# Linear attention followed by a gated MLP: fewer dummy matmuls and another VectorE order in the prologue, and phi(q) of batch 1 taken in the given layout ahead of full-width transposes

## The chip, the cores and the metric

The kernel runs on one core of one Trainium2 chip. The metric is the device time of one execution in microseconds.

## The reference, cut to what matters

```python
# q, k, v: (8, 8, 576, 64) float32
def phi(x):
    return np.where(x > 0, x, np.exp(x) - 1.0) + 1.0      # = max(x, 0) + min(exp(x), 1)
q_p, k_p = phi(q), phi(k)
kv  = np.einsum('bhsd,bhse->bhde', k_p, v)
z   = np.sum(k_p, axis=2)
num = np.einsum('bhsd,bhde->bhse', q_p, kv)
den = np.einsum('bhsd,bhd->bhs', q_p, z)[..., None] + 1e-06
x   = (num / den).transpose(0, 2, 1, 3).reshape(4608, 512)
g   = x @ w_gate                                          # 512 -> 1536
out = ((g * sigmoid(g)) * (x @ w_val)) @ w_out            # 1536 -> 512
```

## The kernel before: what the change and the argument touch

Tokens are worked off in nine groups of 512, "layer 1" being gate and value (L292), "layer 2" the output product (L299). Batch 0's attention has no matmuls of another group to hide behind: it is the prologue. Batch 1's is woven into layer 2 of the first group. TensorE needs q with the features on the partitions, so q is transposed on TensorE. For batch 0 that is a matmul against the identity into PSUM that already holds 1, then an exponential and one VectorE operation from PSUM:

```python
WARM = (4, 3, 4, 4, 2, 1, 2, 2)        # dummy matmuls of a constant at eight places
def warm(n, w=512, ps=None):           # L124
    for _ in range(n):
        nc.tensor.matmul(out=(ps or pp4[1][1])[:, 512 - w:512], lhsT=ones[:, :],
                         rhs=ones[:, 0:1].to_broadcast([P, w]), start=True, stop=True)
# ... prologue; exp_* run on ScalarE, mx_/mn_/add_/q_phi/zr_copy/r_copy on VectorE
    q_turn(0, qa)                      # L430, 16 half-width turns
    q_exp(0, 0, qa)
    q_exp(0, 1, qa)
    warm(WARM[1])
    q_turn(1, qb)
    q_exp(1, 0, qb)
    q_exp(1, 1, qb)
    warm(WARM[2])
    exp_k(0, 0)
    exp_k(0, 1)
    q_phi(0, 0, qa)                    # L442, 128x512 from PSUM
    q_phi(0, 1, qa)
    mx_k(0, 0)                         # L143, 128x1152
    q_phi(1, 0, qb)
    mn_k(0, 0)                         # L147, 128x1152
    mx_k(0, 1)
    zt(0, 0, X[1], kp, True, False)    # L396, column sums of kp on TensorE, 9 matmuls
    warm(WARM[3])
    zt(0, 0, X[1], ek, False, True)    # column sums of ek: need mn_k(0, 0)
    zr_copy(0, 0, X[1])                # L400
    warm(WARM[4])
    t_corners(0, Zr, 0, pp4[2])        # denominators
    lnrd(pp4[2], 0)                    # 1/den by Ln and Exp on ScalarE
    mn_k(0, 1)
    q_phi(1, 1, qb)
    zt(0, 1, Y[0], kp, True, False)
    warm(WARM[5])
    zt(0, 1, Y[0], ek, False, True)
    add_k(0, 0)                        # L159, 128x1152
    zr_copy(0, 1, Y[0])
    warm(WARM[6])
    kv_corner(0, 0, kp, True, True)    # L185
    # ... r_copy, the second half, xT, then layer 1
```

For batch 1, raw q is transposed in 64-column halves and phi is taken after, from PSUM:

```python
    def qtr(b, lp, ps):                                      # L371, 16 halves
        pt = ps[:, :].bitcast(FP16).rearrange("p (j c) -> p j c", c=P)
        for j in range(J - 1):
            for l2 in range(2):
                nc.tensor.transpose(out=pt[D * l2:D * l2 + D, j, :],
                                    in_=qr[b][:, 2 * lp + l2, D * j:D * j + D], identity=id16[:, :])
    def t_phi(a, ps):
        return (lambda: act(a, ps, AF.Exp),
                lambda: nc.vector.tensor_scalar(out=a, in0=a, scalar1=1.0, scalar2=None, op0=ALU.min),
                lambda: nc.vector.scalar_tensor_tensor(out=a, in0=ps, scalar=0.0, in1=a,
                                                       op0=ALU.max, op1=ALU.add))   # L385
    # ... layer2_0
        def s0(): qtr(1, 0, cq[0]); exp_k(1, 1); pm[0][0](); mn_k(1, 1); add_k(1, 1)
                  zsum(1, 1, 2); pm[0][1](); pm[0][2]()
        def s1(): # qtr8 (L379, 8 halves of the ninth slot, both batches), then their phi
        def s3(): qtr(1, 1, cq[1]); pm[1][0]()
        def s5(): p1_z(); pm[1][1](); pm[1][2]()
        step = {1: [s0], 4: [s1, s3], 5: [s5]}
        for fb in range(9):
            for f in step.get(fb, []): f()
            for t in range(4): l2_mm(0, t, fb)               # L299
        s4()                                                 # L254: denominators of batch 1
```

(The step functions are shortened to one line each, and `s4`, which holds the denominators, is only named.)

## Time and profile before

| | before |
|---|---|
| time, median of 3 | 315.97 us (315.6 to 316.2) |
| span of the profiled run | 314.1 us |
| TensorE busy | 307.5 us, 98% |
| VectorE, ScalarE busy | 205.5 us (65%), 152.0 us (48%) |
| start of layer 1's long run of L292 | 19.64 us |
| first L299 of layer 2, and first L299 after the denominators L254 | 36.91 and 46.99 us |

The lines themselves stand in the prediction below. They are to be read thus. A TensorE that is busy for 98% leaves 2%: 2.4 us of it in the first 15 us, and 4.1 us after 309 us, when only the last tiles and the last store are left. But in the prologue TensorE is fed with dummies, so the busy share says nothing there. What sets the time there is the chain of work: each line of it gives a start, a length and what ran, and each piece began when the one above released it. Two numbers of the chain: the start of the column sums on `ek` (L396, L398 after the change), called E, and the start of layer 1's long run of L292, called L.

### The profile page before, as it was taken

Reading aid. Unit: us, or ns where it says so; the run is one execution under the profiler, and the core shown is the slowest. Engines: PE = TensorE matmul, PEld = TensorE weight load, DVE = VectorE, ACT = ScalarE, POOL = GpSimd, SP = SyncE. Lnnn points to the kernel's source line nnn. Section 1 sums busy time; section 2 is a strip of 40 time slices with the busy share of each in tenths; the row PEclk is TensorE's granted clock in tenths of the full one; section 3 lists DMA queues with packets and bytes.
Section 4 is the critical chain, followed back from the end, with each engine's and each line's share of the span. In section 5 each row is a group of like instructions: output and inputs, shape, how many; then the busy total and the mean of one; then the engine's idle time right before and its main releaser. Section 6 shows DMA issues by size and latency. Waiting matters only on the chain.

```text
span 314.1 us, 5531 instructions
## 1 busy us (share of the span) xinstructions
PE 307.5 (98%) x2186; PEld 142.7 (45%) x2186; DVE 205.5 (65%) x362; ACT 152.0 (48%) x231; POOL 48.0 (15%) x72
## 2 busy tenths in 40 slices
PE   8899999999999999999999999999999999999994
PEld 4444444444544454445444544444444444444442
DVE  4854688899789767977597849874991434133410
ACT  4865839738643745366535743475330333133311
POOL 7755334300000230023000500000000000000000
PEclk9999999999999999999999999999999999999999
DMA  8999999995612396129702990314032400140014
GB/s 216 198 198 199 206 207 232 238 206 88 140 33 41 50 180 170 38 41 163 197 20 57 134 230 0 75 35 102 0 61 59 91 1 1 37 98 0 2 33 100
DMA packets 41162, 32.80 MB, mean 104 GB/s; under 512 B 16432, under 2 KB 36144, under 8 KB 41136
## 3 DMA queue, kind: packets, MB, share of 16 engines
q0 software_dynamic: 20464, 18.29, 37.2%
q1 hardware_dynamic: 20592, 14.13, 18.6%
q8 instruction: 17, 0.28, 0.4%
q14 instruction: 9, 0.07, 0.1%
q10 hardware_dynamic: 80, 0.03, 0.0%
HBM read 37.75 MB, written 9.44 MB: 150 GB/s over the span
## 4 chain that ended last, share of the span: by engine, by line
PE 96%; DMA 1%; DVE 1%; ACT 1%; issue 0%
PE pp L292 57%; PE pp L299 30%; PE pp L276 2%; PE pp L254 2%; PE pp L185 2%; DMA q<-in_q_dram 1%; PE pp L124 1%; PE pp L430 1%; ACT qT L120 0%; ACT ek L120 0%; PE pp L371 0%; PE pp L396 0%; DVE kp L159 0%; PE pp L212 0%; DVE ek L147 0%; DVE osb L322 0%
## 5 line engine op out<-in xcount | busy, mean ns | idle before, releaser
L120 ACT ACTIVATE sil<-pp 128x512 f16<-128x512 f32 x108 | 63.4, 597 | 101.8 <-PE pp L292 100.9
L292 PE MATMUL pp<-xT,wg 128*128 128x512 f16 x416 | 106.8, 379 | 0.0
L292 PE MATMUL pp<-xT,wv 128*128 128x512 f16 x416 | 106.8, 379 | 0.0
L285 DVE SCALAR_TENSOR_TENSOR hT<-pp,sil 128x512 f16<-128x512 f32 x108 | 72.4, 682 | 49.0 <-PE pp L292 35.6
L299 PE MATMUL pp<-wo,hT 128*128 128x512 f16 (+2 forms) x444 | 97.2, 374 | 0.6 <-DVE osb L322 0.6
L299 PEld LDWEIGHTS <-hT 128*128 128x128 f16 x444 | 41.9, 98 | 49.7 <-issue 2.1
L292 PEld LDWEIGHTS <-wv 128*128 128x128 f16 x416 | 40.7, 98 | 49.1
L292 PEld LDWEIGHTS <-wg 128*128 128x128 f16 x416 | 40.7, 98 | 48.4
L322 DVE TENSOR_SCALAR osb<-pp 128x512 f32<-128x512 f32 (+1 forms) x19 | 12.9, 682 | 30.6 <-PE pp L299 26.2
L120 ACT ACTIVATE osb<-pp 128x512 f32<-128x512 f32 (+1 forms) x18 | 10.3, 573 | 34.8 <-PE pp L299 34.8
L120 ACT ACTIVATE ek<-kr 128x1152 f16<-128x1152 f16 x16 | 17.8, 1156 | 0.1
L120 ACT ACT_TABLE_LOAD x13 | 16.7, 1283 | 2.3 <-PE pp L292 2.1
L693 POOL COPY gate<-qT 128x1 f16<-128x1 f16 x4 | 1.3, 320 | 97.9 <-DVE hT L285 71.2
L229 DVE TENSOR_TENSOR qp<-qp,rden 128x1152 f16<-128x1152 f16 x12 | 16.2, 1347 | 0.0
L220 DVE TENSOR_REDUCE den<-prod 128x18 f32<-128x1152 f16 x12 | 16.1, 1344 | 0.0
L271 DVE TENSOR_SCALAR xT<-pp 128x512 f16<-128x512 f32 (+1 forms) x14 | 8.8, 667 | 7.1 <-PE pp L254 7.1
L120 ACT ACTIVATE eq<-qr 128x1152 f16<-128x1152 f16 x12 | 13.2, 1147 | 0.0
L103 POOL DMA_DIRECT2D vr<-in_v_dram x16 | 11.7, 735 | 9.3 <-PE pp L292 3.5
L103 POOL DMA_DIRECT2D kr<-in_k_dram x16 | 11.7, 735 | 7.8 <-DMA wo<-in_moe_w_out_dram 1.8
L147 DVE TENSOR_SCALAR ek<-ek 128x1152 f16<-128x1152 f16 x16 | 7.7, 483 | 7.5 <-ACT ek L120 7.5
L159 DVE TENSOR_TENSOR kp<-ek,kp 128x1152 f16<-128x1152 f16 x16 | 12.1, 758 | 0.5
L103 POOL DMA_DIRECT2D qr<-in_q_dram x14 | 10.1, 723 | 5.8 <-DMA wo<-in_moe_w_out_dram 1.8
(76 smaller groups left out, 183.6 us busy)
## 6 DMA issues: line engine op xcount, KB each, us to landing
out_dram<-osb SPq DMA_DIRECT2D x70, 128.0 KB, 3.2
kr<-in_k_dram POOLq DMA_DIRECT2D x16, 288.0 KB, 8.9
vr<-in_v_dram POOLq DMA_DIRECT2D x16, 288.0 KB, 9.8
qr<-in_q_dram POOLq DMA_DIRECT2D x14, 288.0 KB, 12.1
wo<-in_moe_w_out_dram POOLq DMA_DIRECT2D x3, 512.0 KB, 12.7
wg<-in_moe_w_gate_dram POOLq DMA_DIRECT2D x5, 256.0 KB, 9.1
wv<-in_moe_w_val_dram POOLq DMA_DIRECT2D x5, 256.0 KB, 9.7
q<-in_q_dram SPq DMA_DIRECT2D x2, 576.0 KB, 4.1
```

The lines of the kernel that those rows point to most:

```text
L103: nc.gpsimd.dma_start(out=dst[b % NB][:, 2 * lp:2 * lp + 2, :], in_=src[b].rearrange("(l a) (c j) d -> (a c) l (j d)", a=2, j=J)[:, 2 * lp ...
L120: nc.scalar.activation(out=out, in_=in_, func=func, bias=bias, scale=scale)
L147: nc.vector.tensor_scalar(out=a, in0=a, scalar1=1.0, scalar2=None, op0=ALU.min)
L159: nc.vector.tensor_tensor(out=a, in0=ek[b % 2][:, lp, :, :], in1=a, op=ALU.add)
L185: nc.tensor.matmul(out=ps[hh][D * l2:D * l2 + D, D * lp:D * lp + D], lhsT=t[b % 2][rows, lp, j, D * l2:D * l2 + D], rhs=vr[b % NB][rows, 2 ...
L220: nc.vector.tensor_reduce(out=den[:, c, :], in_=prod[:, :, :].rearrange("p j (l d) -> p (j l) d", d=D), axis=AX.X, op=ALU.add)
L229: nc.vector.tensor_tensor(out=qv, in0=qv, in1=rden[:, c, :].unsqueeze(2).to_broadcast([P, 2 * J, D]), op=ALU.mult)
L271: nc.vector.tensor_scalar(out=dst, in0=ps[l2][:, c0:], scalar1=1.0 / SC, scalar2=None, op0=ALU.mult)
L285: nc.vector.scalar_tensor_tensor(out=hT[g % 2][:, fb, :], in0=ps[1][:, :], scalar=SC, in1=s[:, :], op0=ALU.mult, op1=ALU.mult)
L292: nc.tensor.matmul(out=ps[h][:, :], lhsT=w[:, c, P * fb:P * fb + P], rhs=xT[g % 2][:, c, :], start=(c == 0), stop=(c == 3))
L299: nc.tensor.matmul(out=l2p[(g, t)][:, n0:n1], lhsT=hT[g % 2][:, fb, P * t:P * t + P], rhs=wo[:, fb, n0:n1], start=(fb == 0), stop=(fb == F ...
L322: nc.vector.tensor_scalar(out=o[:, n0:n1], in0=ps[:, n0:n1], scalar1=1.0 / SC, scalar2=None, op0=ALU.mult)
```

## The change

There are two parts. In the prologue, two of three dummies ahead of the turning of q's second half are dropped (and one added where TensorE waits anyway), so that ScalarE gets to the exponential of k earlier; VectorE takes the last quarter of phi(q) before k's min, and a max of k later. In batch 1, phi(q) is taken before the transposing, on plain fp16 data in SBUF. Then one transpose can take two heads at once (128x128, no mode change), the result is only copied (by ScalarE, the ninth slot by VectorE), and most of one of two column sums goes from VectorE (`zsum`) to TensorE (nine matmuls of width 2).

```diff
-    WARM = (4, 3, 4, 4, 2, 1, 2, 2)
+    WARM = (4, 1, 4, 5, 2, 1, 2, 2)
 ...
-    def qtr(b, lp, ps): ...            # 16 halves from raw q
+    def turn(lp, ps):
+        pt = ps[:, :].bitcast(FP16).rearrange("p (j c) -> p j c", c=P)
+        for j in range(J - 1):
+            nc.tensor.transpose(out=pt[:, j, :], in_=qp[1][:, lp, j, :], identity=id16[:, :])
+        act(qT[1][:, lp, 0:8, :, :].rearrange("p j h c -> p (j h c)"), ps[:, :].bitcast(FP16))
 ...                                    # + mx_p, add_p, phi_q8, turn8
+    def copy8(b, ps):
+        nc.vector.tensor_copy(out=qT[b][:, :, 8, :, :].rearrange("p l h c -> p l (h c)"),
+                              in_=ps[:, 256 * b:256 * b + P].bitcast(FP16)...)
 ...
     q_phi(1, 0, qb)
+    q_phi(1, 1, qb)
     mn_k(0, 0)
-    mx_k(0, 1)
 ...
     lnrd(pp4[2], 0)
+    mx_k(0, 1)
     mn_k(0, 1)
-    q_phi(1, 1, qb)
 ...
     def p1_z():
-        for lp in range(2): ...         # two sums, both on zs
+        ps = b1p["z"][1]
+        nc.tensor.matmul(out=ps[:, 0:2], lhsT=zs[:, 0, 0, :], rhs=ob[:, 0:P:C], start=True, stop=True)
+        for j in range(J):
+            nc.tensor.matmul(out=ps[:, 2:4], lhsT=kp[1][:, 1, j, :], rhs=ob[:, 0:P:C],
+                             start=(j == 0), stop=(j == J - 1))
 ...
         def s0():
-            qtr(1, 0, cq[0])
+            act(eq[0][:, :, D * 8:D * 9], qr[0][:, :, D * 8:D * 9], AF.Exp)
             exp_k(1, 1)
-            pm[0][0]()
+            exp_q(1, 0); exp_q(1, 1); phi_q8(); mx_p(0)
             mn_k(1, 1)
             add_k(1, 1)
-            zsum(1, 1, 2)
-            pm[0][1](); pm[0][2]()
+            mn_q(1, 0); add_p(0); mx_p(1); mn_q(1, 1); add_p(1)
         def s1():
-            qtr8(dz[0]); ...
+            turn(0, cq[0])
         def s3():
-            qtr(1, 1, cq[1]); pm[1][0]()
-        def s5(): p1_z(); pm[1][1](); pm[1][2]()
+            turn(1, cq[1]); turn8(...) x4; p1_z(); copy8(0, dz[0]); copy8(1, dz[0])
-        step = {1: [s0], 4: [s1, s3], 5: [s5]}
+        step = {1: [s0], 6: [s1], 8: [s3]}
```

(Calls that stand on lines of their own are joined here.) The changed kernel has two lines more above the prologue, so L396, L400, L412, L430 and L442 of before are L398, L402, L414, L432 and L444 after.

More of the change, by code (lines that the diff above doesn't have):

```diff
@@ L363 @@
         nc.vector.memset(ob[C * h:C * h + C, C * h:C * h + C], 1.0)
-    def qtr(b, lp, ps):
+    def turn(lp, ps):
         pt = ps[:, :].bitcast(FP16).rearrange("p (j c) -> p j c", c=P)
         for j in range(J - 1):
-            for l2 in range(2):
-                nc.tensor.transpose(out=pt[D * l2:D * l2 + D, j, :], in_=qr[b][:, 2 * lp + l2, D * j:D * j + D],
-                                    identity=id16[:, :])
-    def qtr8(ps):
-        pt = ps[:, :].bitcast(FP16).rearrange("p (b i c) -> p b i c", i=4, c=P)
-        for b in range(2):
-            for lp in range(2):
-                for l2 in range(2):
-                    nc.tensor.transpose(out=pt[D * l2:D * l2 + D, b, lp, :],
-                                        in_=qr[b][:, 2 * lp + l2, D * 8:D * 9], identity=id16[:, :])
@@ L382, in t_phi @@
-    def t_phi(a, ps):
-        return (lambda: act(a, ps, AF.Exp),
-                lambda: nc.vector.tensor_scalar(out=a, in0=a, scalar1=1.0, scalar2=None, op0=ALU.min),
-                lambda: nc.vector.scalar_tensor_tensor(out=a, in0=ps, scalar=0.0, in1=a, op0=ALU.max, op1=ALU.add))
-    def t_phi_main(b, lp, ps):
-        return t_phi(qT[b][:, lp, 0:8, :, :].rearrange("p j h c -> p (j h c)"), ps[:, :].bitcast(FP16))
-    def t_phi_8(b, ps):
-        return t_phi(qT[b][:, :, 8, :, :].rearrange("p l h c -> p l (h c)"),
-                     ps[:, 256 * b:256 * b + P].bitcast(FP16).rearrange("p (l c) -> p l c", l=2))
+            nc.tensor.transpose(out=pt[:, j, :], in_=qp[1][:, lp, j, :], identity=id16[:, :])
@@ new lines, in turn, with mx_p, add_p, turn8 @@
+        act(qT[1][:, lp, 0:8, :, :].rearrange("p j h c -> p (j h c)"), ps[:, :].bitcast(FP16))
+    def mx_p(lp):
+        nc.vector.tensor_scalar(out=jl(qp, 1, lp), in0=lj(qr, 1, lp), scalar1=0.0, scalar2=None, op0=ALU.max)
+    def add_p(lp):
+        nc.vector.tensor_tensor(out=jl(qp, 1, lp), in0=jl(qp, 1, lp),
+                                in1=eq[1][:, hs(lp), :].rearrange("p l (j d) -> p l j d", d=D), op=ALU.add)
+    def turn8(b, lp, ps):
+        pt = ps[:, :].bitcast(FP16).rearrange("p (b i c) -> p b i c", i=4, c=P)
+        nc.tensor.transpose(out=pt[:, b, lp, :], in_=qp[b][:, lp, 8, :], identity=id16[:, :])
@@ new lines, in copy8, with phi_q8 @@
+    def copy8(b, ps):
+        nc.vector.tensor_copy(out=qT[b][:, :, 8, :, :].rearrange("p l h c -> p l (h c)"),
+                              in_=ps[:, 256 * b:256 * b + P].bitcast(FP16).rearrange("p (l c) -> p l c", l=2))
+    def phi_q8():
+        r, e = qr[0][:, :, D * 8:D * 9], eq[0][:, :, D * 8:D * 9]
+        nc.vector.tensor_scalar(out=r, in0=r, scalar1=0.0, scalar2=None, op0=ALU.max)
+        nc.vector.tensor_scalar(out=e, in0=e, scalar1=1.0, scalar2=None, op0=ALU.min)
+        nc.vector.tensor_tensor(out=qp[0][:, :, 8, :].rearrange("p a (l d) -> p a l d", d=D),
+                                in0=e.rearrange("p (a l) d -> p a l d", l=2),
+                                in1=r.rearrange("p (a l) d -> p a l d", l=2), op=ALU.add)
@@ L524, in p1_z @@
     def p1_z():
-        for lp in range(2):
-            ps = b1p["z"][1]
-            nc.tensor.matmul(out=ps[:, 2 * lp:2 * lp + 2], lhsT=zs[:, lp, 0, :], rhs=ob[:, 0:P:C],
-                             start=True, stop=True)
+        ps = b1p["z"][1]
[3 more added lines that the diff above has]
+                             start=(j == 0), stop=(j == J - 1))
         nc.vector.tensor_scalar(out=Zr[1][:, :, :, :].rearrange("p l h e -> p (l h) e"),
@@ L580, in layer2_0 @@
         cq, dz = b1p["q"], b1p["z"]
-        p8 = [t_phi_8(b, dz[0]) for b in range(2)]
-        pm = [t_phi_main(1, lp, cq[lp]) for lp in range(2)]
         nc.scalar.preload_act_table_set("natural_log_exp_and_others")
@@ L593, in s0 @@
         def s0():
-            qtr(1, 0, cq[0])
+            act(eq[0][:, :, D * 8:D * 9], qr[0][:, :, D * 8:D * 9], AF.Exp)
             exp_k(1, 1)
-            pm[0][0]()
+            exp_q(1, 0)
+            exp_q(1, 1)
+            phi_q8()
+            mx_p(0)
             mn_k(1, 1)
             add_k(1, 1)
-            zsum(1, 1, 2)
-            pm[0][1]()
-            pm[0][2]()
+            mn_q(1, 0)
+            add_p(0)
+            mx_p(1)
+            mn_q(1, 1)
+            add_p(1)
         def s1():
-            qtr8(dz[0])
-            for f in (0, 1, 2):
-                for b in range(2):
-                    p8[b][f]()
+            turn(0, cq[0])
         def s3():
-            qtr(1, 1, cq[1])
-            pm[1][0]()
-        def s5():
+            turn(1, cq[1])
+            for b in range(2):
+                for lp in range(2):
+                    turn8(b, lp, dz[0])
             p1_z()
-            pm[1][1]()
-            pm[1][2]()
+            for b in range(2):
+                copy8(b, dz[0])
         def s4():
```

## The prediction

> **What bounds the kernel now.** I read the page's engine row first, then TensorE's waits, then the chain of work that ended last, and last the timeline of the two stretches that the change touches.
>
> ```profile
> PE 307.5 (98%) x2186; PEld 142.7 (45%) x2186; DVE 205.5 (65%) x362; ACT 152.0 (48%) x231; POOL 48.0 (15%) x72
> PE 96%; DMA 1%; DVE 1%; ACT 1%; issue 0%
> ```
>
> TensorE matmuls are recorded as busy for 98% of the span and carry 96% of the chain. Part of that is padding: 22 matmuls of a constant (L124) in the first 20 us, so a stretch can be "busy" and still wait. The waits of PE, all of them:
>
> ```profile
> PE pp L124 <- DVE ones L355: 1.1, 1, 1.1
> PE pp L396 <- DVE ek L147: 0.8, 1, 0.8
> PE pp L299 <- DVE osb L322: 0.6, 1, 0.6
> PE pp L185 <- DVE kp L159: 0.3, 1, 0.3
> PE pp L430 <- DVE qr L448: 0.2, 1, 0.2
> ```
>
> Four of the five fall before 15 us, one at 309 us; none lies between 15 and 309. The change touches the prologue (batch 0's attention, to about 19.6 us) and layer 2 of the first group (36.7 to 51.3 us, into which batch 1's attention is woven). From 51 us on the instruction order is the same on every engine and PE runs through, so what is gained or lost before 51 us should arrive at the end one for one. The chain in order of time, prologue:
>
> ```profile
> 6.23 0.76 PE pp L124 x3
> 6.99 0.61 PE pp L430 x12
> 7.62 1.26 ACT qT L120 x2
> 8.88 1.06 ACT ek L120
> 9.97 0.66 DVE ek L147
> 10.67 0.39 PE pp L396 x9
> ```
>
> Columns: start, length, what. Three dummies delay the turning of q's second half (L430), the two exponentials of it delay the exponential of k, that delays k's min on VectorE, and that delays the column sums L396. VectorE then becomes the limit:
>
> ```profile
> 11.67 0.69 DVE L442 SCALAR_TENSOR_TENSOR qT<-pp,qT 128x512 f16<-128x512 f32 x1
> 12.27 0.75 DVE L159 TENSOR_TENSOR kp<-ek,kp 128x1152 f16<-128x1152 f16 x1
> 13.07 0.48 PE L185 MATMUL pp<-vr,kp 64*64 64x64 f16 x36
> ```
>
> The last phi of q (L442) sits ahead of the add (L159) that releases L185. In layer 2, TensorE has these foreign pieces between its 0.216 us matmuls:
>
> ```profile
> 37.70 0.64 PE L371 MATMUL pp<-id,qr 128*64 128x128 f16 x16
> 40.97 0.41 PE L379 MATMUL pp<-id,qr 128*64 128x128 f16 x8
> 41.22 0.61 PE L371 MATMUL pp<-id,qr 128*64 128x128 f16 x16
> 46.23 0.76 PE L254 MATMUL pp<-qT,Zr 64*64 64x64 f16 x16
> 46.92 1.47 PE L299 MATMUL pp<-wo,hT 128*128 128x512 f16 x6
> ```
>
> **What the Trainium skill says.** "TensorEngine Tiling (Array Packing)", section Key Properties: changing the tiling mode drains TensorE; its section Restrictions: column tiling switches Fast Weight Load off. The trace agrees: four L299 from 36.75 at 0.216 would let the next start at 37.61, and the 128*64 transposes start at 37.70; before L379 it is 40.86 against 40.97. Their weight loads take 110 ns for 64 columns, full ones 97 to 98 ns for 128. "VectorE: DVE Perf Modes", section on the perf-mode tier table: a copy with a PSUM operand gets at most 2x, a two-tensor op with one 1x. The 128x1024 scalar_tensor_tensor from PSUM took 1225 ns, near one element per cycle; no copy of 16-bit PSUM data is in this trace, so the 2x is untested. "ScalarE: Activation LUTs", section What ACT_TABLE_LOAD costs: 186 ns plus 0.833 ns per element for an activation with immediates; the trace's 1152-wide exponentials took 1147 to 1162 ns against 1146. "TensorE: Matmul & The Clock Gate", Part 1: the clock falls to half after an idle window of about 3.4 us; the trace shows only the rise (four dummies in 1.89 us at the start, three in 0.82 us at 6.16).
>
> **Part 1, the prologue.** Two dummies go ahead of the second turning: 2 x 0.216 = 0.43 us. The first half of that turning can start at about 6.47, but its second half needs the last cast, which ends at 6.19 + 0.58 = 6.77. Eight transposes at 0.73/16 = 0.045 us are through by then; four more from 6.85 plus about 0.2 of latency give 7.25. ScalarE is free at 5.99 + 1.26 = 7.25. So its two exponentials start at about 7.27 instead of 7.62: 0.35 gained, and exp of k ends at about 9.6 instead of 9.94. VectorE now does L442 for the last quarter before k's min: L143 from 7.93, L442 from 8.34 and 8.97, so the min can start at 9.61, the same moment: gain 0.36. One more dummy at this place (five for four) only fills a wait: after it PE would still idle about 0.4.
> The column sums then end about 0.37 earlier and Zr (L400), no longer behind the second L143 by issue order, follows them at once; the denominators reach ScalarE at 11.52 instead of 11.89. On VectorE: Zr 10.73 to 11.02, L143 to 11.4, L147 to 11.8, then the add 11.75 to 12.5 where it was 12.27 to 13.02. So L185 starts about 0.52 earlier (12.55), and r_copy, the second add and the second L185 follow with 0.52. The ending is a race: the last xT products (L412 at 17.01) wait for L254 (16.50, would be 15.97) and for ScalarE's chain of eight Ln and Exp, which runs on from 11.52 and hands over at about 16.6. The first product needs only its half. L276's third chunk (17.76) therefore comes 0.40 to 0.53 earlier. I take 0.45. No weights stand in the way: the issuing engine's waits put the landing of the second wv block at 18.5 us and its first use at 20.1.
>
> **Part 2, PE work in layer 2.** Removed: 32 L371 and 8 L379 with their drains. Before: 38.27 - 37.61 = 0.66, 41.76 - 40.86 = 0.90, and 0.07 for the two L527, together 1.63 us. Added: 16 + 4 full transposes, ten column sums of width 2. A full weight load with a 128-wide matmul is in this trace: the last twelve L299 take 0.83 us, of which 0.17 + 0.05 is the last one's own length, so 0.055 each. 20 x 0.055 = 1.10. The sums follow L396: 0.30/9 = 0.033 each, 0.33. Sum 1.43, and no mode changes: 0.20 less.
>
> **Part 3, the waits that this creates there.** In before's time scale: ScalarE's table load ends at 37.98. Then exp of 256 columns (186 + 213 = 0.40, overlapping 0.06 with the next as the pairs in the trace do), exp k to 39.48, exp q to 40.57 and 41.66. VectorE: min k 39.51 to 39.97, add 40.01 to 40.77, min q (0.46) to 41.17, add (0.76) to 41.97, so the first eight transposes can start at 42.03. PE arrives there after 24 L299: 36.75 + 24 x 0.2158 = 41.93. Wait 0.10. The second eight have their data at 43.56 and PE arrives at 44.20: none.
> The second wait is at L254: its output overwrites the two banks which Zr and the two slot-8 copies read, so it waits for VectorE. PE: transposes 44.20 to 44.86, sums to 45.19, four L299 to 46.05, mode change, 46.14. VectorE: Zr (0.42) from 45.38 to 45.80, then two 256-wide copies. At 2x an estimate from that page's table is (120 + 128)/0.96 = 0.26 each; at 1x they would be like L385's 0.38 to 0.42. L254 starts at 46.27 or 46.50. Before it started at 46.23 but paused about 0.1 in its middle for the last qT. So layer 2 resumes at 46.87 to 47.10 against 46.92: -0.05 to +0.2. The 0.20 of PE work is eaten by the wait for the copies. I take +0.05. The four zsum operations (1.2 us) and the two long L385 leave VectorE, whose load there was not the limit.
>
> **Sum.** 315.97 - 0.45 + 0.05 = 315.6 us.
>
> **Rivals.** (a) The prologue's gain is lost: the turning waits for the last cast as a whole (its weight load is listed with 0.4 us of wait for L451). Then it starts at 6.85 instead of 6.92, the front gains 0.07, and only the reorder on VectorE helps; ScalarE's denominators would come 0.1 earlier: about 315.9. Against it: the 0.42 us gap is what every mode change shows here, and the listed order waits for that cast only at the ninth transpose. (b) Full transposes run slower than the 128-wide matmuls at the end, say 0.08: +0.5 us, 316.1. For it: transposes in full mode are nowhere in the trace. (c) Everything fits: no wait at the first transposes, 2x copies, full 0.53 in the prologue: 315.3. (d) Fewer dummies let the clock drop: the gaps would stay below 0.5 us each, far from 3.4; if it dropped, some 3 us at half rate would cost 1 to 2 us. Unlikely. (e) A load comes late, as PE is earlier: q's second half of batch 1 lands at 40.0 by the issue waits and its exponential would start at 40.1 after the shift; it has 0.6 us of slack behind it.
>
> **Range and chances.** The runs of before spread over 0.6 us. My parts are uncertain by about 0.2 and 0.3. Range 315.1 to 316.2. Two per cent is 6.3 us, thirty times what is at stake: 0.98 for within, 0.01 for either side.
>
> **What would show it.** Right: k's min starts near 9.6, L185 near 12.55, layer 1's first L292 near 19.0 (19.48 before); the full transposes at 0.055 apart in one run of eight; a PE wait on VectorE of 0.1 to 0.4 just before L254 at about 45.8. Wrong: ScalarE's third exponential still near 7.6 (a), transposes at 0.08 apart (b), a PE wait of over 0.5 us ahead of the first transposes (a mistake in the ScalarE or VectorE queue), or any PEclk digit below 9 after 8 us.

## The result, and the profile after

| | before | after |
|---|---|---|
| median, fast runs of the same rounds | 316.06 us (4 runs) | 315.32 us (4 runs, 315.0 to 315.34) |
| ratio, 95% interval | | 0.9977 (0.9959 to 0.9994) |
| span of the profiled run | 314.1 | 313.2 |
| E, L | 10.67, 19.64 | 10.13, 19.07 |
| first L299 to first L299 after L254 | 10.08 | 9.86 |

A ratio is the mean time of one kernel's fast runs over the mean of the other's in the same rounds, so it is not quite the ratio of the medians. Within 2%, and inside the predicted range. A later repeat of the same pair in another job gave 0.9991 (0.9979 to 1.0003), told below as the run r_after: the two estimates are 0.7 and 0.3 us, and the interval of the second just includes no gain at all.

The page of the changed kernel, engine row (busy us, share of the span, instructions):

```profile
PE 307.0 (98%) x2173; PEld 142.7 (46%) x2173; DVE 203.8 (65%) x361; ACT 154.0 (49%) x232; POOL 46.9 (15%) x72
```

Thirteen TensorE instructions fewer, 0.5 us less of its time; VectorE gave 1.7 us, ScalarE took 2.0. None of these shows where the end moved. The waits of PE in the changed kernel, the row that was 0.8 before:

```profile
PE pp L398 <- DVE ek L147: 0.2, 1, 0.2
```

This row fell by 0.6, but 0.2 us of that fall were bought with the dummy added just ahead of it: a dummy fills a wait and shortens nothing. The chain of work of the changed kernel:

```profile
6.76 1.19 DVE qT L444 x2
...
8.41 1.20 DVE qT L444 x2
9.61 0.47 DVE ek L147
...
10.13 0.39 PE pp L398 x9
...
12.57 0.48 PE pp L185 x36
...
19.07 17.27 PE pp L292 x80
36.34 5.18 PE pp L299 x24
41.52 0.50 PE pp L370 x8
...
43.74 0.45 PE pp L370 x8
...
44.42 0.24 PE pp L530 x9
...
45.57 0.64 PE pp L254 x16
46.20 1.40 PE pp L299 x6
```

and the counterparts of the kernel before, in its chain of work:

```profile
13.09 0.53 PE pp L185 x36
...
19.64 17.27 PE pp L292 x80
36.91 0.86 PE pp L299 x4
...
46.99 1.40 PE pp L299 x6
```

The chain no longer goes through the exponentials on ScalarE but through four phi(q) on VectorE; the min L147 begins at 9.61, as predicted. (It is a tie: ScalarE's exponential ended at 9.58.) L is 0.57 earlier, the resumption of L299 0.79 earlier. From there on the two kernels stay 0.73 to 0.83 apart (at the start of the last twelve L299: 309.80 and 308.97), so what was gained before 51 us does arrive at the end.

One length in it was not in the prediction: the min took 0.64 us before. The timeline of the kernel before (start, length, engine, line, operation):

```profile
9.61 0.74 POOL L112 DMA_DIRECT2D wv<-in_moe_w_val_dram  x1 [0.66 <-DMA kr<-in_k_dram]
9.97 0.64 DVE L147 TENSOR_SCALAR ek<-ek 128x1152 f16<-128x1152 f16 x1 [0.94 <-ACT ek L120]
```

and of the kernel after, with the two copies of slot 8:

```profile
9.61 0.46 DVE L147 TENSOR_SCALAR ek<-ek 128x1152 f16<-128x1152 f16 x1
9.64 0.74 POOL L112 DMA_DIRECT2D wv<-in_moe_w_val_dram  x1 [0.67 <-DMA kr<-in_k_dram]
...
45.03 0.48 DVE L385 COPY qT<-pp 128x256 f16<-128x256 f16 x2
```

The same operation took 0.64 when it began 0.36 us after GpSimd had begun to issue a load, and 0.46 when it began ahead of that. So of the 0.54 us by which E moved in this pair, 0.36 are the predicted ones and 0.18 are luck of the meeting. The pair of copies took 0.48 us, 0.24 from one to the next.

### The profile page after: what moved, and what is told of

It is laid out like the page before. It is cut to its first block, busy times and chain, and to the rows that moved or that the text cites. A ratio compares the mean times of both kernels' runs of the same rounds, so it can differ in the third digit from the quotient of the medians.

```text
span 313.2 us, 5502 instructions
## 1 busy us (share of the span) xinstructions
PE 307.0 (98%) x2173; PEld 142.7 (46%) x2173; DVE 203.8 (65%) x361; ACT 154.0 (49%) x232; POOL 46.9 (15%) x72
## 4 chain that ended last, share of the span: by engine, by line
PE 95%; DVE 2%; DMA 1%; SPq 0%; issue 0%; ACT 0%
PE pp L292 57%; PE pp L299 30%; PE pp L276 2%; PE pp L254 2%; PE pp L185 2%; DMA q<-in_q_dram 1%; DVE qT L444 1%; PE pp L124 1%; PE pp L398 0%; PE pp L370 0%; DVE kp L159 0%; PE pp L212 0%; DVE osb L322 0%; DVE ek L147 0%; SPq L333 0%; DVE qr L452 0%
## 5 line engine op out<-in xcount | busy, mean ns | idle before, releaser
L299 PE MATMUL pp<-wo,hT 128*128 128x512 f16 (+2 forms) x444 | 97.1, 373 | 0.6 <-DVE osb L322 0.6
L299 PEld LDWEIGHTS <-hT 128*128 128x128 f16 x444 | 42.0, 98 | 49.8 <-issue 2.1
L120 ACT ACTIVATE osb<-pp 128x512 f32<-128x512 f32 (+1 forms) x18 | 10.3, 574 | 34.8 <-PE pp L299 34.8
L120 ACT ACTIVATE eq<-qr 128x1152 f16<-128x1152 f16 (+1 forms) x15 | 15.9, 1099 | 0.3 <-DMA qr<-in_q_dram 0.3
L159 DVE TENSOR_TENSOR kp<-ek,kp 128x1152 f16<-128x1152 f16 x16 | 12.1, 758 | 0.5
L147 DVE TENSOR_SCALAR ek<-ek 128x1152 f16<-128x1152 f16 x16 | 7.5, 470 | 5.4 <-ACT ek L120 5.4
```

The lines of the kernel that those rows point to most:

```text
L120: nc.scalar.activation(out=out, in_=in_, func=func, bias=bias, scale=scale)
L159: nc.vector.tensor_tensor(out=a, in0=ek[b % 2][:, lp, :, :], in1=a, op=ALU.add)
L299: nc.tensor.matmul(out=l2p[(g, t)][:, n0:n1], lhsT=hT[g % 2][:, fb, P * t:P * t + P], rhs=wo[:, fb, n0:n1], start=(fb == 0), stop=(fb == F ...
```

## The experiments

Twelve runs were made (eleven edits and the changed kernel again), in three jobs on three chips; all gave correct outputs. The six kernels that ran once have no spread of their own, so their time is given but not argued from. This table has the readings of every profile, from its chain of work: E, L, their difference (the rest of the prologue), and the stretch from the first L299 to the first L299 after the denominators.

| kernel | dummies, order | batch 1 | E | L | L − E | layer-2 stretch | 16 first turns |
|---|---|---|---|---|---|---|---|
| before | old, old | old | 10.67 | 19.64 | 8.97 | 10.08 | 1.37 |
| after | new, new | new | 10.13 | 19.07 | 8.94 | 9.86 | 0.89 |
| r_after | new, new | new | 10.35 | 19.29 | 8.94 | 9.87 | 1.50 |
| e1_dummies | new, old | old | 10.23 | 19.19 | 8.96 | 10.28 | 0.89 |
| e2_order | old, new | old | 10.59 | 19.52 | 8.93 | 10.09 | 1.14 |
| e3_prologue | new, new | old | 10.35 | 19.39 | 9.04 | 10.08 | 0.89 |
| e4_batch1 | old, old | new | 10.31 | 19.29 | 8.98 | 9.98 | 1.05 |
| e6_slow_copy8 | new, new | slow copies | 10.14 | 19.08 | 8.94 | 10.35 | 0.89 |
| e9_sums_early | new, new | sums earlier | 10.43 | 19.36 | 8.93 | 9.77 | 1.50 |
| e11_tail_dummies | two fewer, new | new | 10.50 | 19.29 | 8.79 | 9.95 | 0.89 |
| e8_kfirst | other, k first | new | 9.95 | 19.03 | 9.08 | 9.87 | 1.50 |
| e5_halves | new, new | half transposes | 10.49 | 19.42 | 8.93 | 10.71 | 0.89 |
| e7_zsum | new, new | sums on VectorE | 10.45 | 19.38 | 8.93 | 11.00 | 1.18 |
| e10_best | fewer, k first | sums earlier | 9.86 | 18.56 | 8.70 | 9.77 | 1.05 |

The last column is the length of the same sixteen turnings of q's first half. They are identical in every kernel, and ran from 0.89 to 1.50 us. At the start TensorE goes at half pace: dummies stand 427 ns apart and turnings 107 ns, later 217 and 56 ns. The pace changes before these turnings (after), within them (before) or behind them (r_after, e9). The row of the granted clock shows 9 at both paces, so that a clock coming up is the reason is the prediction's reading and not shown. The first k half landed at different times too: its max L143 waited for the load until 8.15 to 8.46 in e2, e4, e5, e7, e8, e10 and r_after, while in the other seven profiles it had landed between 7.24 and 7.97. Both shift E by some tenths with no edit at all: e4 has the prologue of before, unedited, and its L is 19.29 against 19.64. So one profile against another proves no 0.3 us in E; L − E and the layer-2 stretch are the firmer readings.

The theory was the prediction's own: dummies 0.36, the order another 0.15 at L185, layer 2 about even. The rivals: that the order alone does it, that the dummies' gain is swallowed by a wait, and that the gain comes from batch 1.

**e1_dummies: the dummy counts alone.**

```diff
-    WARM = (4, 3, 4, 4, 2, 1, 2, 2)
+    WARM = (4, 1, 4, 5, 2, 1, 2, 2)
```

> The kernel before with the changed dummy counts alone (two fewer ahead of the second turning of q, one more ahead of the second column sums). My theory (each of the two prologue edits takes away a different wait, and the dummies' one lies first): q's third exponential starts near 7.3 us instead of 7.62, k's min near 9.6 instead of 9.97, layer 1's first L292 0.35 to 0.45 us earlier than 19.48, the time 0.3 to 0.5 us below the kernel before. Rival A (VectorE's order is the only limit, as the changed kernel's chain runs through L444 on VectorE): L292 moves by less than 0.1 us. Rival B (a different phase of the clock's rise at the start, not the edit: the first sixteen transposes took 0.89 us after and 1.37 us before): the start of L292 follows the length of the first transposes, not the edit.

Measured: median 315.42, ratio 0.9995 (0.9982 to 1.0007). E 10.23, 0.44 earlier than in before's profile, with the old order of VectorE; the min began at 9.67. Rival B holds in part: from the start of the first turnings to q's third exponential it is 2.30 to 2.37 us with the new dummies and turnings of 0.89, 2.66 with turnings of 1.50 (r_after, e9), and with the old dummies 2.44 (e4, turnings of 1.05) to 2.76 (before, 1.37). At a like pace the edit still gains 0.12 (e4 against e10) and 0.33 (e2 against e7). The expected 0.3 to 0.5 us did not show in the time, which leaves it open; the layer-2 stretch of this profile was 10.28, because two of VectorE's operations met a load issue (L147 at 38.74 took 0.61, L384 at 44.35 took 0.67) and the chain went through VectorE there.

**e2_order: the VectorE order alone.**

```diff
     q_phi(1, 0, qb)
+    q_phi(1, 1, qb)
     mn_k(0, 0)
-    mx_k(0, 1)
 ...
     lnrd(pp4[2], 0)
+    mx_k(0, 1)
     mn_k(0, 1)
-    q_phi(1, 1, qb)
```

> The kernel before with VectorE's order alone changed (phi of q's last quarter ahead of k's min, k's second max after Zr). My theory: k's min stays near 9.97 us (ScalarE sets it), but the add that releases L185 starts near 12.05 instead of 12.27, so the first L292 comes 0.15 to 0.25 us earlier than 19.48. Rival A (order is everything): 0.5 us or more. Rival C (order is worth nothing without the dummies' edit): below 0.05 us.

Measured: 315.72, ratio 1.0002 (0.999 to 1.0015): nothing in time, where 0.15 to 0.25 us had been expected. Its chain of work:

```profile
10.59 0.39 PE pp L396 x9
...
19.52 17.27 PE pp L292 x80
```

The difference is 8.93, against 8.97 in before and 8.96 in e1. The order brings no 0.15 us behind E. What it does is to make room: with the dummies gone, the last phi(q) ahead of k's min and the exponential of k end together.

**e3_prologue: both.** The edit is the two diffs above.

> The kernel before with both prologue edits and batch 1 as before. My theory: first L292 at 18.9 us like the changed kernel (0.57 earlier than before), the time 0.5 to 0.6 us below before. The rival that the batch 1 part helped the prologue too (through loads, say) expects a later L292 than the changed kernel's 18.91.

Measured: 315.30, ratio 0.9988 (0.9976 to 1.0), E 10.35, L − E 9.04: L came 0.25 us ahead of before's instead of the expected 0.57. Here the min began at 9.59, as in after, but GpSimd's issue had begun at 9.29, and the min took 0.70. The predicted start came true and a quarter of a microsecond was lost in the next operation.

**e4_batch1: the batch 1 part alone** (the changed kernel with `WARM` and the VectorE order of before).

> The changed kernel with the prologue's dummies and order of before: the batch 1 part alone. My theory: L292 at 19.48 us as before, and layer 2 of the first group takes 0.2 us less from its first matmul to its resumption after L254 (9.96 instead of 10.17 us); time 0.15 to 0.3 us below before. The step on record had put this part at +0.05 (range -0.05 to +0.2): if that was right after all and the gain of the whole came from the prologue, this run is not faster in that stretch.

Measured: 315.58, ratio 0.9999 (0.9986 to 1.0011). The layer-2 stretch was 9.98, 0.10 under before's. Its first transposes waited some 0.17 because VectorE's max of q (L374 at 38.70) took 0.66, again 0.31 us after the start of a load issue (38.39). In time the three single parts are all inconclusive: the interval of each is wider than what is looked for.

**e6_slow_copy8: are the two copies what L254 waits for?** The copies are made slow on purpose, with the same result: a two-tensor operation that multiplies by ones.

```diff
-        nc.vector.tensor_copy(out=qT[b]..., in_=ps[...])
+        nc.vector.scalar_tensor_tensor(out=qT[b]..., in0=ps[...], scalar=1.0,
+                                       in1=ones[:, :].unsqueeze(1).to_broadcast([P, 2, P]),
+                                       op0=ALU.mult, op1=ALU.mult)
```

> The changed kernel with the two slot-8 copies from PSUM done as products with a tile of ones (same result, but a two-tensor operation). In the changed kernel the two copies took 0.48 us together and L254 started about 0.1 us after PE was ready for it. My theory (those copies end the wait ahead of L254): the pair takes 0.76 us as the two 256-wide operations of before did, L254 comes 0.25 to 0.3 us later after the fourth L299, and the stretch from layer 2's first piece in the chain to the piece after L254 grows from 9.86 to 10.10 to 10.15 us. Rival (PE's own change of tiling mode is what L254 waits for): no change beyond 0.05.

Measured, one run: 315.59. Its timeline:

```profile
45.27 0.74 DVE L386 SCALAR_TENSOR_TENSOR qT<-pp,ones 128x256 f16<-128x256 f16 x2
46.07 0.64 PE L254 MATMUL pp<-qT,Zr 64*64 64x64 f16 x16 [0.29 <-DVE qT L386]
```

The pair took 0.74 instead of 0.48. From the four L299 ahead of L254 to L254 it was 1.32 us (44.75 to 46.07), against 1.05 in after (44.52 to 45.57): 0.27 more for 0.26 more of copying. So L254 starts when VectorE is done with the copies, and their speed counts one for one. That a mode change would set this gap instead is refuted. The whole stretch rose by 0.49, as the first transposes of this run waited 0.23 too (L155 was stretched to 0.68).

**e9_sums_early: the column sums one step earlier**, so that Zr is made before the copies are due.

```diff
-            p1_z()                     # in s3
-        step = {1: [s0], 6: [s1], 8: [s3]}
+        step = {1: [s0], 6: [s1], 7: [p1_z], 8: [s3]}
```

> The changed kernel with batch 1's column sums and Zr moved one step ahead (step 7 instead of 8), so that only the two copies lie behind the last transposes. My theory: the wait ahead of L254 goes, the stretch shrinks from 9.86 to about 9.76 us (the change of mode stays). Rival (mode change alone): 9.86 stays, or it grows if the ten small matmuls cost more there.

Measured, one run: 315.28; the stretch 9.77, the wait ahead of L254 gone. That is 0.09 below after, about the wait of 0.10 that could be won. From the four L299 to L254 it is now 0.96 us (44.80 to 45.76): four times 0.216 and a gap of 0.10, as it stands ahead of the 128*64 transposes of before (0.09 and 0.11). So a change of mode costs 0.10 here, and the copies cost what comes on top.

**e11_tail_dummies: what sets L − E?** The changed kernel without the two dummies ahead of L185.

```diff
-    WARM = (4, 1, 4, 5, 2, 1, 2, 2)
+    WARM = (4, 1, 4, 5, 2, 1, 0, 2)
```

> The changed kernel without the two dummies ahead of the first L185. In all six profiles so far the time from the second half of the column sums (on ek) to layer 1's first long run was 8.93 to 9.04 us, with the VectorE order changed or not, so my step that the order brings 0.15 us there has fallen; in the changed kernel the add that releases L185 ended at 12.25 and L185 began at 12.50. New theory (PE's own remaining dummies set this stretch): 8.94 falls to about 8.7 to 8.75. Rival (ScalarE's eight Ln and Exp set it): it stays at 8.94, and the last xT products still start at 6.3 after those sums.

Measured, one run: 315.39; E 10.50, L − E 8.79, the shortest so far. Its chain of work:

```profile
12.00 0.68 DVE kp L159
12.72 0.55 PE pp L185 x36
...
19.29 17.27 PE pp L292 x80
```

and from its timeline the copy of Zr:

```profile
12.59 0.28 DVE L402 TENSOR_SCALAR Zr<-pp 128x128 f16<-128x128 f32 x1
```

With the dummies gone the add L159 on VectorE releases L185. In after the add ended at 12.25 and L185 only began at 12.50: TensorE was working off its own dummies. (The profile of after names another releaser of L185, the copy Zr that ended at 12.45. It is not one: here L185 began at 12.72 while that copy ran until 12.87.) This is why the better order gained nothing behind E. It did bring the end of the add forward, from 2.35 us after E in before to 2.12 in after, but L185 began 2.40 and 2.37 after E: the dummies were the limit there, and VectorE was no longer.

**e8_kfirst: a different way to an early E.** The exponential of k goes between the two of q's second half; k's min goes ahead of the last phi(q).

```diff
     q_exp(1, 0, qb)
+    exp_k(0, 0)
     q_exp(1, 1, qb)
     warm(WARM[2])
-    exp_k(0, 0)
 ...
     q_phi(1, 0, qb)
-    q_phi(1, 1, qb)
     mn_k(0, 0)
+    mx_k(0, 1)
 ...
     lnrd(pp4[2], 0)
-    mx_k(0, 1)
+    q_phi(1, 1, qb)
     mn_k(0, 1)
```

and `WARM = (4, 1, 4, 3, 2, 1, 2, 2)`.

> The changed kernel with the exponential of k's first half moved ahead of the fourth exponential of q on ScalarE, k's min ahead of q's last quarter on VectorE, and two dummies fewer while PE waits for it. Theory (ScalarE's and VectorE's queues tie at 9.6 us in the changed kernel, and q's last quarter isn't needed yet): the min starts at 9.1 to 9.3 if k's first half has landed by 7.9, later by as much as it lands later; the sums on ek start 0.3 to 0.5 earlier than 10.13, and the 8.94 after them stays. Rival (k's loads set it): the min starts 1.1 us after a late landing, no gain.

Measured, one run: 315.03. Its chain of work:

```profile
8.23 1.17 ACT ek L120
9.95 0.39 PE pp L398 x9
```

The exponential of k started 0.02 us after k had landed (8.21), so E cannot go much lower without an earlier load. E is 0.40 below r_after, which had the same slow first turns (1.50); L − E is 9.08, 0.14 worse and not the expected 8.94, as the displaced phi(q) delays the second min (TensorE's sums on it waited for VectorE at 11.69). Net 0.26.

The last job ran these four on one chip with the kernel before in its rounds (eleven runs, median 315.55).

**r_after: the changed kernel again.** No edit.

> The changed kernel again, on the same chip as the others of this call. The runs of the kernel before spread over 1.1 us in one earlier call (315.03 to 316.13), and its prologue's events move by 0.3 us and more with no edit. Theory: the mean gain is 0.3 to 0.8 us. Rival (the first measurement, 0.0023 of the time, was a lucky draw, as the prologue part alone gave 0.0012 and the batch 1 part 0.0001): under 0.3 us.

Measured: 315.27 (6 runs, 314.98 to 315.76), ratio 0.9991 (0.9979 to 1.0003). E 10.35 and L 19.29, 0.22 later than in the first profile of the very same kernel; L − E and the layer-2 stretch are the same to 0.01 (8.94 and 9.87). The gain lies on the border of the two expectations (0.28 us by medians, 0.31 by means). Its chain of work starts at another place, the landing of k's first half (1.35 + 6.80 = 8.15; in after it landed at 7.92):

```profile
1.35 6.80 DMA kr<-in_k_dram
...
9.83 0.47 DVE ek L147
```

**e5_halves: are full transposes better than halves?** The changed kernel, each 128x128 transpose as two 128x64.

```diff
-            nc.tensor.transpose(out=pt[:, j, :], in_=qp[1][:, lp, j, :], identity=id16[:, :])
+            for l2 in range(2):
+                nc.tensor.transpose(out=pt[D * l2:D * l2 + D, j, :],
+                                    in_=qp[1][:, lp, j, D * l2:D * l2 + D], identity=id16[:, :])
```

(and the same for the ninth slot.)

> The changed kernel with each 128x128 transpose split into two of 128x64 as before had them (same data, same copies). Theory (the full-width transposes are what saves TensorE time, by 0.056 against 2 x 0.036 us and by having no change of mode): each group of eight takes 0.66 from one L299 to the next instead of 0.45, the stretch grows from 9.86 to 10.3 to 10.5 us. Rival (the saving came from VectorE's chain alone): it stays below 10.0.

Measured, one run: 316.19; the stretch 10.71, with 0.37 of it a wait for VectorE (two of its operations were stretched to 0.71 and 0.69 by load issues). Less the 0.37 it is 10.34, 0.48 over after. The sixteen halves took 0.57 for what eight full ones do in 0.45, and a drain of 0.10 stood ahead of them. This run confirms the sign, and its size (9.86 to between 10.3 and 10.5 expected) only after taking off the wait.

**e7_zsum: the column sums back on VectorE** (`zsum(1, 1, 2)` after the add of k, two sums in `p1_z`, placed as in after).

```diff
             add_k(1, 1)
+            zsum(1, 1, 2)
 ...
-        for j in range(J): ...          # nine sums on kp
+        # the second sum on zs, as before
```

> The changed kernel with the second half of batch 1's zsum kept on VectorE (four operations of 1.2 us together) and two column sums on TensorE instead of ten. Theory (VectorE's queue ahead of the first transposes is full, the wait there was 0.05): the first transposes wait 1.2 us more, TensorE saves 0.25, the stretch grows from 9.86 to 10.7 to 10.9 us. Rival (there is slack): no growth, as the nine small matmuls go.

Measured, one run: 316.31; the stretch 11.00. The waits of PE in it:

```profile
PE pp L370 <- DVE qp L377: 1.2, 1, 1.2
```

Four small VectorE operations (about 1.2 us) ahead of phi(q) become a 1.2 us wait of TensorE at the first transposes. In the kernel before the same four cost little, but VectorE was not idle there: L254 paused about 0.1 us for the last phi(q), and in e1, where two operations of that queue were stretched, the chain ran through it. Moving the sums to TensorE is what makes this layout possible: nine sums for 0.24 us instead of 1.2.

**e10_best: what pointed beyond both kernels, in one.** e8's order with the add of k earlier, the dummies of e8 less the two that e11 took, and e9's sums.

```diff
-    WARM = (4, 1, 4, 5, 2, 1, 2, 2)
+    WARM = (4, 1, 4, 3, 2, 1, 0, 2)
 ...                                    # e8's order, and:
     lnrd(pp4[2], 0)
+    add_k(0, 0)
     mn_k(0, 1)
+    q_phi(1, 1, qb)
 ...
+        step = {1: [s0], 6: [s1], 7: [p1_z], 8: [s3]}
```

> The changed kernel with the three edits that helped so far together (exponential and min of k's first half first, no dummies ahead of the first L185, column sums of batch 1 one step ahead), and k's first add and second min ahead of q's last quarter on VectorE. Theory: the sums on ek at 9.6 to 10.0 us as k's landing has it, 8.6 to 8.8 us from there to layer 1's long run (8.94 before, 9.08 with k first alone, 8.79 with the dummies alone), and 9.77 us for layer 2's stretch: in all 0.3 to 0.6 us below the changed kernel. Rival (the loads of k or ScalarE's Ln and Exp bind at once): less than 0.2 us below it.

Measured: 314.41 (314.15 to 314.57), ratio to before 0.9962 (0.995 to 0.9974). Its chain of work:

```profile
9.86 0.40 PE pp L398 x9
...
18.56 17.27 PE pp L292 x80
...
45.59 1.40 PE pp L299 x6
```

E 9.86, L − E 8.70 and the stretch 9.77 are each as low as any profile has. It lies 0.9 us below the changed kernel of the same rounds, by means (314.39 and 315.30), more than the 0.3 to 0.6 that I had expected. Its profile is 0.83 ahead of r_after's at the resumption (45.59 against 46.42): 0.49 from E, 0.24 from L − E, 0.10 from layer 2. The 0.49 is not a matter of the load: k's first half landed at 8.12 here and at 8.15 in r_after. All five runs of it lie below all runs of the changed kernel.

## Why the prediction was right or wrong

The time (315.6 predicted; 315.32 and 315.27 measured) and the sum were right: −0.40 predicted, and the 27 runs of before have the mean 315.68, the 10 of the changed kernel 315.28, all jobs together, so −0.40 with a standard error of about 0.1. But its two terms were off in opposite directions, so that the sum fits so well is luck.

**The prologue, predicted −0.45.** In the first pair of profiles L moved by 0.57, but by another way than the prediction had it. That k's min would start at 9.61, and that the chain would tie there between ScalarE and VectorE, was right to the hundredth. That E moved by 0.18 more came from the min's own length (0.64 to 0.46), the meeting with GpSimd. The step "on VectorE … L185 starts about 0.52 earlier" and with it "the ending is a race … 0.40 to 0.53" failed: L185's start moved by 0.52 in the chain (13.09 to 12.57), but as E had moved by 0.54, nothing came from the order. e2 shows this: L − E 8.93 with the new order and old dummies, 8.96 in e1 with the reverse. What I had overlooked is that TensorE's remaining dummies, not the add, stand ahead of L185 in the new kernel; e11 removed two and the stretch fell by 0.15 (8.94 to 8.79).

The term is also smaller on average than the pair shows. Over the profiles with the old dummies (before, e2, e4) L averages 19.48; over eight with the new dummies (after, r_after, e3, e5, e6, e7, e9, and e1, whose old order moved nothing behind E) 19.27. That is 0.21 instead of the predicted 0.45. What takes the rest away can be read from the start of the min in these eight, 9.77 on average. It is 9.59 to 9.67 in after, e1, e3 and e6, as predicted. In r_after, e7 and e5 it is 9.83, 9.94 and 9.98, because k's first half landed at 8.15, 8.34 and 8.38: the new order puts a max and two phi(q), about 1.6 us of VectorE, between that landing and the min. In e9 it is 9.91, as ScalarE came late behind first turnings of 1.50. And in e3 the min itself took 0.70. So the landing of k weighs most. The prediction took before's landing (its L143 "from 7.93") as given, and at a tie nothing was left for a later one; in e4, with the old order, k landed at 8.30 and the min still began at 9.79. With standard deviations of 0.18 over three and 0.14 over eight profiles, 0.21 has a standard error of about 0.11; this is an average, not a proof.

**Layer 2, predicted +0.05 (range −0.05 to +0.2).** Measured −0.22 in the pair, and −0.22 as an average of before, e1, e2 and e3 (10.13) against after, r_after, e4, e8 and e11 (9.91). The mechanism was right, each of its two waits is there, and the size was off. In before's time scale (first L299 at 36.75 in the timeline, 0.58 later than in after) L254 started at 46.15, where I had 46.27 or 46.50 and took the middle. The mis-sized term is the copies: I took the mean of 2x and 1x, and the pair took 0.48 us, 0.24 from one to the next, near the 2x estimate of 0.26. That is 0.12. Another 0.11 is that VectorE could start Zr at 45.27 instead of 45.38: the wait at the first transposes was 0.05 instead of 0.10, and the ten sums took 0.27 instead of 0.33. L254 itself took 0.56 instead of 0.60. Together 0.27, which is the difference between −0.22 and +0.05. e6 is the test of the copies, e9 of the wait, e7 of the sums.

**The rivals.** (b), slow full transposes, fell: eight took 0.45 us, 0.056 each, where 0.055 was predicted. (a), a turning that waits for the cast as a whole, fell: in after it began at 6.39, by the predicted 6.47. (c), everything fits, came true for layer 2 but for waits of 0.05 at the first transposes and 0.10 ahead of L254. (d), a falling clock, is not there: the dummies keep their full pace (five in 1.25 us from 8.71), and every slice of the clock row has the digit 9, though that row did not show the slow start either. (e), a late load, shows only as 0.3 us in which ScalarE waited for q; it had slack behind it, and no wait for a load stands in layer 2's chain.

**What stays open.** Whether the prologue's part is worth 0.2 or 0.4 us in the mean can't be told from these runs; the single parts e1, e2 and e4 each lie within their interval of nothing. How GpSimd's issue delays VectorE is a regularity of all 14 profiles (given at the end), but was not tested by an experiment of its own: no kernel here moved the issues.

## What to carry to other kernels

Dummies that keep TensorE busy, and any entry of an in-order queue, hide the wait that they fill: before crediting a better order, look at which of the near-tied limits (an engine's queue, a landing, padding) still holds. When two paths are brought to a tie, ask how late each event ahead of them can come: here a load that varied by a microsecond took part of the gain. When runs scatter by 1 us and the effect is 0.3, measure the stretch between two fixed events in several profiles, and don't trust one pair. Doing the elementwise work in the given layout, transposing at full width and only copying out of PSUM pays where VectorE's queue has been emptied first, here by giving column sums to TensorE.

## What the Trainium skill lacked or had wrong

- "SBUF — State Buffer", section Who interferes with whom, says that a VectorE operation in a two-port mode and GpSimd exclude each other for the whole instruction of whichever issues first. These traces agree that one waits for the other, and show where in an issue the lock falls, which the page lacks. The 1152-wide fp16 max and min take 0.44 to 0.46 us alone. When one began within the first 0.25 us of a load issue of GpSimd, it took no longer, and many of these issues took longer, up to 0.98 us instead of some 0.70 to 0.76. When it began over 0.28 us after the start of an issue and over 0.21 us before its end, it ended 0.26 us after that end (0.28 to 0.29 where the next issue followed at once), in all 51 cases of the 14 profiles, and so took up to 0.73 us. In before: 9.61 + 0.74 = 10.35, and the min ended at 10.61. So GpSimd seems to take the lock some 0.25 us into its issue and to keep it to the end, while the first 0.2 us of the waiting operation still pass beside it (argued from the records, not tested).
- "TensorE: Matmul & The Clock Gate", Part 4: PE-mode transpose, gives some 275 to 390 ns for one 128x128 transpose and says that the full clock doesn't engage for them. Here one fp16 transpose is recorded with 0.22 us, eight in a row among other matmuls took 0.45 us, 0.056 each, and four more 0.22. That is the pace of the prologue's turnings after the slow start (56 ns; 107 before), so in a stream of matmuls they ran at full pace. The page lacks the rate of transposes in a row.
